# Two attentions in one kernel: the last 64 projected rows of A with high and low weights side by side in one stationary tile

## The chip, the cores and the metric

One core of a Trainium2 chip. The metric is the device time of one execution in microseconds, as the median of several runs. A core has TensorE (PE, with its weight loads PEld), VectorE (DVE), ScalarE (ACT), GpSimd (POOL) and SyncE (SP, which issues most DMAs here). TensorE's products go to eight PSUM banks of 128 partitions x 512 float32; ACT and VectorE read them there, GpSimd works on SBUF alone in this kernel.

## The reference

Two attention blocks of the same size (2048 positions, width 576, 32 heads of 18) stand beside each other in the output: A looks at eight earlier positions in steps of two, B at all.

```python
def _A_ref(x, wqkv, wo):
    qkv = (lambda x, *d: x.transpose(*d))((x @ wqkv).reshape(B, S, 3, H, Dh), 2, 0, 3, 1, 4)
    q, k, v = qkv[0], qkv[1], qkv[2]
    ...
    kg = k[:, :, idx_c, :].reshape(B, H, S, W, Dh)
    vg = v[:, :, idx_c, :].reshape(B, H, S, W, Dh)
    logits = jnp.einsum("bhsd,bhswd->bhsw", q, kg) * scale
    logits = jnp.where(mask[None, None, :, :], logits, -1e9)
    attn = _softmax(logits, axis=-1)
    o = jnp.einsum("bhsw,bhswd->bhsd", attn, vg)
    return (lambda x, *d: x.transpose(*d))(o, 0, 2, 1, 3).reshape(B, S, D) @ wo
...
a = _A_ref(A_x, A_wqkv, A_wo)
b = _B_ref(B_x, B_wqkv, B_wo)
return jnp.concatenate([a, b], axis=-1)
```

The change lies in A's `x @ wqkv`: 1728 output columns (q, k and v of 576 each) for 2048 positions, with a contraction over 576.

## The kernel before

**Products of two parts.** The projections are float32 products made from a high and a low part of each operand: `hi` is the value rounded to `float32r`, `lo` the rest. Each product is taken as high x high, high x low and low x high. `split` (L428) makes both parts: ACT copies to `hi`, another engine subtracts to get `lo`. The contraction of 576 is four pieces of 128 and a last one of 64; for the last, `xhl` holds the high part of x in one half of the partitions and the low part in the other, and the weights stand in both halves (`whh` high, `wll` low, each twice).

**A's projected rows.** The 1728 output columns of A are cut into 14 chunks of 128, chunk 13 having only 64. A chunk's weights are the stationary operand, 512 positions of x move, and the result (128 or 64 rows x 512 positions) is stored to the DRAM tensor `da`, from which A's attention reads q, k and v. `chunk(c)` (L472) makes a chunk's loads (`get`, `get_last`: queue SP) and splits (`put`, `put_last`: ACT, then GpSimd). Two rooms, `a0` for even chunks and `wp` for odd ones from 2 on, each hold one chunk's weights (tiles `ahi`, `alo` of 128x512 and `ahh`, `all` of 128x128). `leave_a` (L713) takes a finished product out: ACT copies the bank to a tile `ohi`, SP stores that to `da`.

**The stream.** `stream` (L344) runs the products of a work list of 92 in groups of four and four turns a group. It cuts each contraction in two halves of the rows: half r=0 uses partitions 0 to 63, half r=1 partitions 64 to 127, and TensorE works on an instruction of each half at the same time. `halves` (L324) lists the pieces of one half: 4 x 3 of the 128-row pieces and one or two of the last, 14 where the half is the one that holds the low rest (`odd`), else 13. In turn 0 of a group half 0 works on product 0 and half 1 on product 1, in turn 1 on 2 and 3; in turns 2 and 3 each half does the other's products into the same banks, so that two halves never write one bank together. After turn 2 products 0 and 1 leave, after turn 3 products 2 and 3. The four banks of the ring "scores" hold a group's products.

**Maxima among the products.** B's softmax needs row maxima of its scores. `maximum` (L240) computes a 128x512 piece of scores on TensorE (L161) into a bank of the ring "else" (three banks) and lets VectorE reduce it (L169). The stream takes 258 such pieces per half along for later. `most(j)` says how many are given out by the end of turn j; `stream` spreads the turn's share evenly over the turn's instructions of each half. Turns 0 to 11 are products for B's v; from turn 12 on the share is 237 pieces in 80 turns. The last turn (j = 91) also carries four scores (L285) of the main part, whose exponentials ACT makes (L293); they use the ring "else" too. The last turn's list begins with them: score, maximum, score in each half.

**Order by hand.** Schedules are lists of functions by turn number: `at(n, ...)` in the projection, run by `slot()` at the end of a turn; chunk k from 4 on is loaded at turn index 36 + 4k - 2 and split at 36 + 4k and 36 + 4k + 1, some four turns ahead of its use. `posts` are small transfers of finished maxima into `qs` (L200, queue SP). The chunks run in the order of the work list: chunks 0 and 1 by pairs of x blocks, then 2 to 13 with all four x blocks, one group each. Chunk 13 is the last group, j = 88 to 91. After the stream comes the main part: 511 steps of four scores, exponentials, maxima for later blocks, and products with v (`weigh`, L763), with A's attention on GpSimd beside them. A bank that is not yet read out makes the instruction that wants to write it wait, and TensorE takes its instructions in order.

Of the kernel before, what the change touches and what calls it, by code (L numbers as in the profile page):

```python
# [7 lines left out]
F32 = mybir.dt.float32  # L8
F32R = mybir.dt.float32r
BF16 = mybir.dt.bfloat16  # L10
AF = mybir.ActivationFunctionType
# [50 lines left out]
def two_attentions(ctx: ExitStack, tc, xa, wa, woa, xb, wb, wob, out):  # L62
# [265 lines left out]
        return [(b[at], a[at]) if weights_move else (a[at], b[at]) for a, b in both]  # L328


    ctx.enter_context(tc.manual_schedule())
    make_set(stack0, 0)

# [10 lines left out]
    def stream(products, most, last):  # L344

        where, ends = {}, {}
        for j in range(len(products)):
            first = j - j % 4
            turn = [((0, 0), (1, 1)), ((0, 2), (1, 3)), ((0, 1), (1, 0)), ((0, 3), (1, 2))][j % 4]
            both = []
            for r, k in turn:
                args, view, _ = products[first + k]
                if j % 4 < 2:  # L360
                    where[k] = view(bank("scores"))
                else:
                    assert sum(given) - ends[k] > 3
                parts = halves(r, *args)
                both.append([(where[k], *ab, j % 4 < 2 and i == 0, j % 4 > 1 and i == len(parts) - 1)
                             for i, ab in enumerate(parts)])
            n = most(j) - given[0]
            others = last if j == len(products) - 1 else ([], [])
            n += 2 if others[0] else 0
            total = n + len(both[0])  # L370
            for r in range(2):
                for i in range(n):
                    both[r].insert((4 * i + 1 + 2 * r) * total // (4 * n), None)
            for pair in zip(*both):
                for r, p in enumerate(pair):
                    if p is None:
                        (others[r].pop(0) if others[r] else maximum(r))()
                    else:
                        ps, a, b, start, stop = p
                        nc.tensor.matmul(ps, a, b, start=start, stop=stop)  # L380
            for k in sorted(k for _, k in turn):
                if j % 4 < 2:
                    ends[k] = sum(given)
                else:
                    products[first + k][2](where[k])
            slot()
            for _ in range(min(len(posts), 2)):
                posts.popleft()()
        do_all(posts)
# [9 lines left out]
    with (tc.tile_pool(name="x", bufs=1, side="right") as xp,  # L399
# [28 lines left out]
        def split(engine, hi, lo, t):  # L428
            nc.scalar.activation(hi, t, AF.Copy)  # L429
            engine.tensor_sub(lo, t, hi)  # L430
# [41 lines left out]
        def chunk(c):  # L472
# [12 lines left out]
                    load(t[1][64 * r : 64 * r + 64, :n], wa[512:, 128 * c : 128 * c + n])  # L485

            def put():
                hi, lo = (a_room(c).tile([128, 512], F32R, name=nm, bufs=1) for nm in ("ahi", "alo"))
                split(nc.gpsimd, hi[:, : 4 * n], lo[:, : 4 * n], t[0][:, : 4 * n])
                w[:2] = ([u[:, n * k : n * k + n] for k in range(4)] for u in (hi, lo))  # L490

            def put_last():
                w[2:] = (a_room(c).tile([128, 128], F32R, name=nm, bufs=1) for nm in ("ahh", "all"))
                split(nc.gpsimd, w[2][:, :n], w[3][:, :n], t[1][:, :n])

            return w, [get, get_last], [put, put_last]

        def a_room(c):
            return a0 if c % 2 == 0 else a1 if c == 1 else wp


# [4 lines left out]
        if True:  # L506
# [195 lines left out]
                    at(gets[c], lambda b=b, c=c: xas[b][1](c))  # L702
                    at(puts[c], lambda b=b, c=c: xas[b][2](c))
            for k in range(2, 14):
                n = 46 if k == 2 else 36 + 4 * k
                if k == 3:
                    at(n, third_rows)
                at(n - 2 if k != 3 else n, *ws[k][1])
                at(n if k != 3 else n + 2, ws[k][2][0])
                at(n if k == 2 else n + 1 if k > 3 else n + 3, ws[k][2][1])  # L710
            at(90, first_room)

            def leave_a(c, b, n, ps):  # L713
                o = xp.tile([128, 512], F32, name="ohi", bufs=4)
                nc.scalar.activation(o[:n], ps, AF.Copy)  # L715
                load(da[128 * c : 128 * c + n, HALO + 512 * b : HALO + 512 * b + 512], o[:n])


            order = [t for i in (0, 8) for j in range(4) for t in (i + j, i + j + 4)]
# [16 lines left out]
                                              lambda ps: ps, lambda ps, i=i, b=b, c=c: leave(i, b, c, ps)))  # L736

            order = [(c, b) for b0 in range(0, NB, 2) for c in range(2) for b in (b0, b0 + 1)]
            order += [(c, b) for c in range(2, 14) for b in range(NB)]
            for c, b in order:  # L740
                n = min(128, 3 * D - 128 * c)
                work_list.append(((b % 2, ws[c][0], xas[b][0], slice(0, n), every),
                                  lambda ps, n=n: ps[:n], lambda ps, c=c, b=b, n=n: leave_a(c, b, n, ps)))

            es = [None] * 4
            few = 7 * (NT - 4) // 4
            turns = len(work_list) - NT + 4
            stream(work_list, lambda j: 7 * (j + 1) // 4 if j < NT - 4 else
                   few - (few - EARLY_PAIRS) * (j - NT + 5) // turns,
                   [[lambda r=r: es.__setitem__(r, score(0, 0, 0, r, "else")), lambda r=r: maximum(r)(),  # L750
                     lambda r=r: es.__setitem__(r + 2, score(0, 0, 0, r + 2, "else"))] for r in range(2)])
        wa_room.close()
# [716 lines left out]
```

## Time and profile before

| | us |
|---|---|
| median of 3 runs | 1582.14 (1580.37 to 1582.5) |
| the profiled execution | 1579.73 |
| its span | 1577.9 |
| TensorE busy / VectorE / ACT / GpSimd | 1569.6 / 1377.1 / 1207.4 / 969.7 |
| the stream's products (L380), first to last start | 81.6 to 409.8 |
| granted TensorE clock | 1.000 |

In rows of instruction groups the columns are: line, engine, operation, out<-in, shapes, count, then busy us and mean ns of one, then the engine's idle time before them and what ended it. In windows: the stretch, its length, busy time of each engine with the count, the granted clock, the share of the DMA engines and GB/s. In the waits: who waited for whom, us in total, times, the longest. In the timeline: start, length, engine, line, operation, tiles, shapes, count, and in brackets the idle time before it. A matmul's or activation's length includes latency, so neighbours overlap: the distance of two starts is what each costs in a row. TensorE counts as busy through nearly all of the stream and the main part; what sets its pace has to be read from counts and distances.

### The profile page before, as it was taken

What the parts mean: (1) busy time and instruction counts of PE and PEld (TensorE: products, weight loads), DVE (VectorE), ACT (ScalarE), POOL (GpSimd) and SP (SyncE); (2) the same over time, 40 slices, a digit from 0 to 9 for tenths busy, and PEclk for the clock granted to TensorE, in tenths of its full rate; (3) what the DMA queues carried; (4) which work ended last, traced back from release to release, by engine and by line L of the source; (5) the groups of instructions that cost most, each with busy time, mean ns of one, the idle gap of its engine ahead of it and who ended that gap; (6) DMA issues with size and microseconds to landing.
All of it is one profiled execution on the core that took longest, in us unless ns stands there. A gap on an engine that the chain in (4) does not pass through costs nothing.

```text
span 1577.9 us, 34942 instructions
## 1 busy us (share of the span) xinstructions
PE 1569.6 (99%) x13272; PEld 966.4 (61%) x13272; DVE 1377.1 (87%) x2333; ACT 1207.4 (77%) x2411; POOL 969.7 (61%) x803
## 2 busy tenths in 40 slices
PE   9999999999999999999999999999999999999998
PEld 7998899999644445445445445444444444545686
DVE  5289999999999999999989999999999999998633
ACT  6424432121799999999999999999999999998654
POOL 2416742210266995995896897897798799682000
PEclk9999999999999999999999999999999999999999
DMA  9948954532312362245325325421721332154311
GB/s 242 240 147 218 270 164 131 138 107 81 62 41 65 73 142 77 64 122 108 75 77 131 89 81 117 120 79 50 149 85 50 91 95 57 51 167 131 140 57 69
DMA packets 188168, 175.65 MB, mean 111 GB/s; under 512 B 119432, under 2 KB 133512, under 8 KB 186272
## 3 DMA queue, kind: packets, MB, share of 16 engines
q1 hardware_dynamic: 182992, 161.73, 37.4%
q0 software_dynamic: 4032, 10.63, 3.3%
q8 instruction: 104, 1.70, 0.5%
q10 hardware_dynamic: 976, 1.07, 0.2%
q14 instruction: 64, 0.52, 0.1%
HBM read 98.77 MB, written 73.47 MB: 109 GB/s over the span
## 4 chain that ended last, share of the span: by engine, by line
PE 93%; DVE 3%; DMA 3%; ACT 1%; SPq 0%; issue 0%; DVEq 0%; ACTq 0%
PE po L766 30%; PE bank L285 19%; PE bank L161 17%; PE bank L380 14%; PE bank L1347 4%; PE bank L1244 3%; PE bank L571 2%; DVE mx L169 2%; PE bank L317 2%; DMA dqk<-ohi 1%; DMA dqk<-olo 1%; DMA qs<-mh 0%; PE bank L1212 0%; ACT e L293 0%; DMA raw<-xa 0%; SPq L530 0%
## 5 line engine op out<-in xcount | busy, mean ns | idle before, releaser
L169 DVE TENSOR_REDUCE mx<-bank 128x2 f32<-128x512 f32 x2048 | 1278.1, 684 | 109.1 <-PE bank L161 81.9
L293 ACT ACTIVATE e<-bank 128x512 f32<-128x512 f32 x2048 | 1047.9, 605 | 80.5 <-PE bank L285 78.0
L161 PE MATMUL bank<-ks,qs 54*128 54x512 f32 (+1 forms) x2464 | 785.8, 380 | 1.6 <-ACT y L1249 0.3
L161 PEld LDWEIGHTS bank<-ks,qs 54*128 54x128 f32 x2464 | 403.2, 184 | 387.6 <-DVE mx L169 341.1
L285 PE MATMUL bank<-qs,ks 56*128 56x512 f32 x2048 | 592.8, 426 | 0.1
L766 PE MATMUL po<-e,v 128*19 128x512 f32 x4096 | 531.7, 599 | 0.5
L285 PEld LDWEIGHTS bank<-qs,ks 56*128 56x128 f32 x2048 | 309.1, 185 | 21.3 <-ACT e L293 14.6
L987 POOL TENSOR_TENSOR pr<-aq,akv 128x1024 f32<-128x1024 f32 x72 | 158.3, 2200 | 16.7 <-PE po L766 13.8
L1029 POOL TENSOR_TENSOR pr<-lg,akv 128x1024 f32<-128x1024 f32 x72 | 158.3, 2198 | 0.6
L766 PEld LDWEIGHTS po<-e,v 128*19 128x19 f32 x4096 | 73.7, 97 | 138.2 <-issue 132.9
L991 POOL TENSOR_TENSOR pr<-pr 128x1024 f32<-128x1024 f32 x64 | 152.6, 2384 | 5.0
L715 ACT ACTIVATE ohi<-bank 128x512 f32<-128x512 f32 (+1 forms) x56 | 30.4, 594 | 149.2 <-issue 134.3
L380 PE MATMUL bank<-xhi,ahi 64*128 64x512 f32 (+1 forms) x448 | 112.9, 386 | 0.0
L380 PE MATMUL bank<-xhi,alo 64*128 64x512 f32 (+1 forms) x448 | 111.7, 387 | 0.0
L380 PE MATMUL bank<-xlo,ahi 64*128 64x512 f32 (+1 forms) x448 | 110.4, 387 | 0.0
L1347 PE MATMUL bank<-wohi,at 64*128 64x288 f32 x480 | 103.3, 305 | 0.0
L1030 POOL TENSOR_TENSOR pr<-pr 128x512 f32<-128x512 f32 x72 | 92.4, 1284 | 5.6
L430 POOL TENSOR_TENSOR alo<-raw,ahi 128x512 fp32r<-128x512 f32 (+1 forms) x14 | 17.6, 1254 | 122.6 <-ACT ahi L429 94.6
L1347 PEld LDWEIGHTS bank<-wohi,at 64*128 64x128 f32 x480 | 74.6, 184 | 27.6 <-ACT e L293 23.8
L525 POOL TENSOR_TENSOR olo<-olo,ohi 128x512 fp32r<-128x512 f32 x36 | 46.2, 1293 | 70.3 <-ACT ohi L524 60.6
L104 POOL CAST mh<-mt 128x32 fp32r<-128x32 f32 x32 | 6.7, 210 | 114.0 <-DVE mt L186 114.0
L1347 PE MATMUL bank<-wolo,at 64*128 64x288 f32 x240 | 70.3, 293 | 0.0
(210 smaller groups left out, 1864.9 us busy)
## 6 DMA issues: line engine op xcount, KB each, us to landing
do<-n SPq DMA_DIRECT2D x30, 512.0 KB
da<-ohi SPq DMA_DIRECT2D x52, 256.0 KB
akv<-da SPq DMA_DIRECT2D x64, 175.5 KB
out<-y SPq DMA_DIRECT2D x31, 288.0 KB
qs<-dqk SPq DMA_DIRECT2D x30, 288.0 KB
ks<-dqk SPq DMA_DIRECT2D x30, 288.0 KB
at<-dao SPq DMA_DIRECT2D x60, 128.0 KB
rec<-drec SPq DMA_DIRECT2D x29, 256.0 KB
```

The costliest lines, as they stand in the source:

```text
L161: return awaiting(nc.tensor.matmul(ps if part is None else ps[:, 256 * r : 256 * r + 256], qs[at, b, p, 128 * t : 128 * t + 128], ks[at, p ...
L169: nc.vector.tensor_reduce(at, ps.rearrange("q (s n) -> q s n", s=2), axis=AX.X, op=ALU.max)
L285: awaiting(nc.tensor.matmul(ps, ks[at, p, 128 * kt : 128 * kt + 128], qs[at, b, p], start=True, stop=True))
L293: nc.scalar.activation(e, ps, AF.Exp, scale=SCALE)
L380: nc.tensor.matmul(ps, a, b, start=start, stop=stop)
L766: nc.tensor.matmul(po[32 * i : 32 * i + 19], vs[g][:, kt, 19 * i : 19 * i + 19], es[i], start=kt == 0, stop=kt == NT - 1)
L987: nc.gpsimd.tensor_mul(pr, ap(st["q"][:, 2 * c], (SUB, 2), (0, W), (1, SUB)), window(st["k"], c))
L991: nc.gpsimd.tensor_add(st["pr"], st["pr"], pr)
L1029: nc.gpsimd.tensor_mul(at, ap(st["lg"], (0, 2), (SUB, W), (1, SUB)), window(st["v"], c))
L1030: nc.gpsimd.tensor_add(at[:, :, :4], at[:, :, :4], at[:, :, 4:])
L1244: nc.tensor.matmul(sums_[r], *both[r][i], start=i == 0, stop=last)
L1347: return nc.tensor.matmul(ps, a, b, start=r == k == 0, stop=r == 1 and k == len(both[1]) - 1)
```

## The change

Chunk 13 has 64 output columns, so its stationary tiles are 64 wide. After the change the high and low weights of that chunk stand side by side in one stationary tile of 128 columns. A piece then has two products (with high x and with low x) where it had three; the high weights' result lands in partitions 0 to 63 of the bank and the low weights' in 64 to 127 (low x low is computed along). Both halves of the bank have to be added: ACT copies one half to its place in `o`, the other to the same rows of a tile `rest`, and GpSimd adds them before the store. The last piece of the contraction is one product instead of one or two.

Chunk 13 changes places with chunk 12 (`a_place`): it is now the last but one group, in room `a0`, and chunk 12 is the last, in room `wp`. Loads and splits follow. `most` is rewritten: the folded turns get two maxima per half each, the other turns share the rest evenly; 258 in all as before.

```diff
+    def folded(r, w, x):
+        both, last = w[:2]
+        at = slice(64 * r, 64 * r + 64)
+        return [(a[at], t[c][at]) for c, a in enumerate(both) for t in x[:2]] + [(last[at], x[2][at])]
...
-                parts = halves(r, *args)
+                parts = folded(r, *args[1:]) if args[0] == "folded" else halves(r, *args)
...
             def put():
+                if folds(c):
+                    t2 = a_room(c).tile([128, 512], F32R, name="ahi", bufs=1)
+                    w[0] = [t2[:, 128 * k : 128 * k + 128] for k in range(4)]
+                    w[2] = a_room(c).tile([128, 512], F32R, name="alo", bufs=1)
+                    split(nc.gpsimd, *(ap(t2[:, n * i :], (2 * n, 4), (1, n)) for i in range(2)), ap(t[0], (n, 4), (1, n)))
+                    return
...
             def put_last():
+                if folds(c):
+                    t2 = w[1] = a_room(c).tile([128, 128], F32R, name="ahh", bufs=1)
+                    split(nc.gpsimd, t2[:, :n], t2[:, n:], t[1][:, :n])
+                    return
...
+        def folds(c):
+            return c == 13
+
+        def a_place(c):
+            return c if c < 12 else 25 - c
+
         def a_room(c):
+            c = a_place(c)
             return a0 if c % 2 == 0 else a1 if c == 1 else wp
...
-                n = 46 if k == 2 else 36 + 4 * k
+                n = 46 if k == 2 else 36 + 4 * a_place(k)
...
             def leave_a(c, b, n, ps):
                 o = xp.tile([128, 512], F32, name="ohi", bufs=4)
-                nc.scalar.activation(o[:n], ps, AF.Copy)
-                load(da[128 * c : 128 * c + n, HALO + 512 * b : HALO + 512 * b + 512], o[:n])
+                at = slice(0, n)
+                if folds(c):
+                    at, other = (slice(64 * r, 64 * r + 64) for r in (b % 2, 1 - b % 2))
+                    rest = ws[c][0][2].bitcast(F32)
+                    nc.scalar.activation(rest[at], ps[other], AF.Copy)
+                    nc.scalar.activation(o[at], ps[at], AF.Copy)
+                    nc.gpsimd.tensor_add(o[at], o[at], rest[at])
+                else:
+                    nc.scalar.activation(o[at], ps[at], AF.Copy)
+                load(da[128 * c : 128 * c + n, HALO + 512 * b : HALO + 512 * b + 512], o[at])
...
-            order += [(c, b) for c in range(2, 14) for b in range(NB)]
+            order += [(c, b) for c in sorted(range(2, 14), key=a_place) for b in range(NB)]
...
-                work_list.append(((b % 2, ws[c][0], xas[b][0], slice(0, n), every),
-                                  lambda ps, n=n: ps[:n], lambda ps, c=c, b=b, n=n: leave_a(c, b, n, ps)))
+                work_list.append((("folded", ws[c][0], xas[b][0]) if folds(c) else
+                                  (b % 2, ws[c][0], xas[b][0], slice(0, n), every),
+                                  lambda ps: ps, lambda ps, c=c, b=b, n=n: leave_a(c, b, n, ps)))
...
-            turns = len(work_list) - NT + 4
-            stream(work_list, lambda j: 7 * (j + 1) // 4 if j < NT - 4 else
-                   few - (few - EARLY_PAIRS) * (j - NT + 5) // turns,
+            folded_ = [args[0] == "folded" for args, _, _ in work_list]
+            plain = [sum(not f for f in folded_[NT - 4 : j + 1]) for j in range(len(work_list))]
+            most = [few + 2 * sum(folded_[:j + 1]) + (EARLY_PAIRS - few - 2 * sum(folded_)) * p // plain[-1]
+                    for j, p in enumerate(plain)]
+            stream(work_list, lambda j: 7 * (j + 1) // 4 if j < NT - 4 else most[j],
```

## The prediction

> **What bounds the kernel now.** I read the page first, then the stage of the change in windows that end where ACT begins to copy a bank out, then that stage's waits, then its last microseconds as a timeline. The page:
>
> ```profile
> span 1577.9 us, 34942 instructions
> PE 93%; DVE 3%; DMA 3%; ACT 1%; SPq 0%; issue 0%; DVEq 0%; ACTq 0%
> L169 DVE TENSOR_REDUCE mx<-bank 128x2 f32<-128x512 f32 x2048 | 1278.1, 684 | 109.1 <-PE bank L161 81.9
> L715 ACT ACTIVATE ohi<-bank 128x512 f32<-128x512 f32 (+1 forms) x56 | 30.4, 594 | 149.2 <-issue 134.3
> ```
>
> TensorE holds 93% of the chain that ended last, so work taken from TensorE should come off the end where TensorE is never kept waiting. Next, the windows restricted to line 380 (`stream`'s products). The first two are one group of four products each, the third is chunk 12, the fourth and fifth are chunk 13's first three turns and its last.
>
> ```profile
> 285.71:300.75 15.04, 15.04 (x110) 14.02 (x110) 1.00 0.64 166
> 300.75:315.55 14.80, 14.80 (x110) 13.86 (x110) 1.00 0.32 100
> ...
> 379.36:394.40 15.04, 15.04 (x111) 13.96 (x110) 1.00 0.21 74
> 394.40:405.95 11.55, 11.55 (x85) 9.45 (x83) 1.00 0.14 48
> 405.95:410.24 4.29, 4.20 (x25) 2.24 (x22) 1.00 0.30 63
> ```
>
> From the code, the two row halves run side by side, and each turn is a row of **slots**: one instruction of each half. A group has 14+14+13+13 = 54 slots of products and, at three maxima per half and turn, 12 more: 66. 15.04/66 = 0.2279 us a slot. The second window is that of a group in which one turn has two maxima per half: 65 slots, and 65 x 0.2279 = 14.81, which is what it took. Two fewer of its 24 reductions would have made it 15.04 x 22/24 = 13.8 if VectorE set the pace. So here **TensorE's slots set the pace**, and VectorE only just follows:
>
> ```profile
> PEld bank L161 <- DVE mx L169: 0.3, 1, 0.3
> 404.57 1.88 DVE L169 TENSOR_REDUCE mx<-bank 128x2 f32<-128x512 f32 x3
> 409.49 1.29 DVE L169 TENSOR_REDUCE mx<-bank 128x2 f32<-128x512 f32 x2 [0.71 <-PE bank L161]
> ```
>
> The waits from 393 to 412 us have TensorE waiting 0.3 us for VectorE. Three reductions in 1.88 us, the last of 0.68, start (1.88-0.68)/2 = 0.60 apart. Six a turn are 3.6 us; a turn is 3.76.
>
> **The change, part by part.** All times are of the profiled execution: 1579.73 us, of which 1577.9 span and 1.83 around it. The runs shown have a median of 1582.14; I take a difference worked out on the one to the other.
>
> *Products.* A folded half has 4 x 2 + 1 = 9 pieces for 13 or 14. With two maxima per half (the new `most`) a folded turn is 11 slots and the group 44. *Maxima.* Their total (258 per half) stays. The old formula gave two instead of three in three of 80 turns: j = 38, j = 65 and the last. The new one gives three in every plain turn but the last, which gets four, so j = 38 and 65 grow by a slot each. *Up to the last turn*, then: old 15.04 + 11.55 = 26.59 us for chunks 12 and 13; new 44 + 2 + 50 (the 17, 17 and 16 slots of chunk 12's first three turns) = 96 slots x 0.2279 = 21.88. **-4.71 us**. Of it 0.16 is that 64-column slots take 11.55/50 = 0.231 us and 128-column ones 0.2279.
>
> The stationary tile gets twice as wide:
>
> ```profile
> L380 PEld LDWEIGHTS bank<-xhi,ahi 64*64 64x64 f32 x31 | 3.7, 132 | 0.2
> L380 PEld LDWEIGHTS bank<-xhi,ahi 64*128 64x128 f32 x38 | 5.7, 186 | 0.0
> ```
>
> The load is 54 ns longer and lies under the other half's and its own previous product: the plain groups pay it in every slot of 0.2279. Were that cover gone, 36 slots x 0.054 = 1.9 us. The Trainium skill's page "TensorE: Matmul & The Clock Gate", section "LDWEIGHTS (loading the stationary operand)", speaks against the change here: a load's time goes with the number of columns, whatever the rows, by its formula 53 ns more for 64 more columns. The two rows agree with it in the difference; a sum that let it show would be 1.9 us higher, and the slots above say that it doesn't show.
>
> *The last turn* changes most. It carries the main part's first four scores (S) among the maxima (M), in the ring of three banks "else". Now:
>
> ```profile
> 405.55 0.54 PE L380 MATMUL bank<-xhi,ahi 64*64 64x512 f32 x2
> ...
> 405.95 1.07 ACT L715 ACTIVATE ohi<-bank 64x512 f32<-64x512 f32 x2 [10.46 <-issue]
> ...
> 406.92 1.07 ACT L293 ACTIVATE e<-bank 128x512 f32<-128x512 f32 x2
> ...
> 407.14 0.69 DVE L169 TENSOR_REDUCE mx<-bank 128x2 f32<-128x512 f32 x1 [0.69 <-PE bank L161]
> 407.56 0.18 PEld L161 LDWEIGHTS bank<-ks,qs 54*128 54x128 f32 x1 [0.48 <-ACT e L293]
> ...
> 407.74 0.28 DVE L179 TENSOR_REDUCE m<-mx 128x16 f32<-128x128 f32 x1
> 408.04 0.18 PEld L285 LDWEIGHTS bank<-qs,ks 56*128 56x128 f32 x1 [0.24 <-ACT e L293]
> ...
> 409.97 0.28 PE L161 MATMUL bank<-ks,qs 54*128 54x256 f32 x1
> ```
>
> It begins at T = 405.55 and the next step at 409.97: 4.42 us for 13 + 4 = 17 slots, which are 3.87; 0.55 is waiting. The order in the ring is S0 S1 M1 M2 S2 S3 M3 M4. M2 needs S0's bank, and S0's exponential queues on ACT behind the two copies of the turn before, until 407.51; hence 407.56, T+2.01. The new last turn has 13 + 6 = 19 slots, 4.33 us, and 12 users of three banks. By the code they stand at slots 0, 2, 3, 5, 7, 8, 10, 11, 13, 15, 16, 18. S0's exponential still ends at T+1.96, so M2, due at 5 x 0.228 = T+1.14, waits until T+2.01: 0.87. Then S2 and S3 go at T+2.5 and 2.7 and M3 at 3.2, and the maxima M3 to M8 come every 0.23 to 0.46 us while VectorE takes one in 0.60. Stepping through with three banks (score to exponential 0.53, exponentials 0.49 apart, maximum to reduction 0.43, bank free at a reduction's end, 0.69), M8 starts at T+5.56 and the turn ends at T+5.79; the same stepping puts the old turn's end at 4.33 against the 4.42 measured, so I add the 0.09: 5.88. **+1.46 us**. Bounds: nothing more than the two slots (+0.46) and, if all of VectorE's eight reductions and the small one follow M2's wait (2.01 + 0.43 + 7 x 0.60 + 0.28, less the old 4.42), +2.5.
>
> *Leaving.* Each folded product is copied by ACT in two halves: eight copies for four, 0.49 us apart (two take 1.07, one 0.59), 2 us more, under the 10.46 us for which ACT was idle before 405.95. A bank is free later, though. With E the end of the third folded turn, copies start at E+0.40; product 1's bank is free at 0.40 + 4 x 0.49 + 0.1 = E+2.46, and the next group first writes it one folded turn later, E + 11 x 0.2279 = 2.51: just in time. GpSimd's sum of two 64x512 halves is not in the trace. Its nearest rows:
>
> ```profile
> L430 POOL TENSOR_TENSOR alo<-raw,ahi 128x256 fp32r<-128x256 f32 x1 | 0.7, 740 | 11.0 <-ACT ahi L429 11.0
> L1030 POOL TENSOR_TENSOR pr<-pr 128x512 f32<-128x512 f32 x72 | 92.4, 1284 | 5.6
> L991 POOL TENSOR_TENSOR pr<-pr 128x1024 f32<-128x1024 f32 x64 | 152.6, 2384 | 5.0
> POOL mh L104 <- DVE mt L186: 29.1, 1, 29.1
> ```
>
> The time goes with the columns, so I take 1.28 (0.74 and 2.38 as bounds). GpSimd does nothing for 29.1 us there. Queued behind the sums are two things. ACT's copy for product 2 reuses the rows of `rest` that the sum for product 0 reads, and product 3's those of product 1: the latter starts at about E + 1.53 + 2 x 1.28 = 4.1 and its bank is free at 5.2, while the second turn of the next group, E + 2.51 + 17 x 0.2279 = 6.39, first needs it. Cover 1.2 us; at 2.38 a sum it would be 1.0 late. SP's stores to `da` wait for the sums, and behind them stand the transfers into `qs` (L200), which belong to blocks that the main part reads only after many steps. Both at 0, up to +1.0.
>
> *Moved.* Chunk 13's load and split take chunk 12's place and the other way round, each a group ahead of its use; the split of chunk 12 (128x512) lands in shorter turns, with 44 slots (10 us) still to go and some 2 us of work. 0.
>
> *Step after the stream.* VectorE comes out of the new last turn with more reductions owed, and the first step needs the banks of M6, M7 and M8. Stepped on, M8's reduction starts at T+6.97 and frees its bank at 7.66; the step's last maximum can go only then, 1.87 after the turn's end. What the step waits for today is ACT, and its last maximum goes beside the score at 411.36, 1.4 after the end:
>
> ```profile
> 410.75 0.57 ACT ohi L715
> 411.36 0.49 PE bank L285
> 411.86 0.99 PE po L766 x8
> ```
>
> The chain goes through the last copy, and that stays put against the end of the stream. I take 0, and keep +0.5. **Sum**: -4.71 + 1.46 = -3.25 us; 1579.73 - 3.25 = 1576.5 for the profiled execution, **1578.9** for the median.
>
> **Rivals.** *The jam goes on* (+0.5 to +1.5): the first step waits for VectorE as well, or ACT's late copies hold a bank in the group after the folded one. For it: the steps behind are TensorE's, so lateness isn't won back. Against: the chain above, and the 1.2 us of cover. -3.25 + 0.9 = -2.35: 1579.8. *No jam*: the exponentials find ACT free, or the ring's order is kinder than my stepping; only the two slots stay: -4.71 + 0.46 = -4.25, 1577.9. Against it: the old turn's 0.55 us, which the stepping gives back within 0.09.
>
> *VectorE is the bound of the stream*, the side where it gets slower. With 0.63 us a reduction (1.88/3) six are 3.78, over a turn's 3.76; then products taken away buy nothing, the number of reductions is the same, and the four put into the last turn cost its +1.46 and the 0.5 behind it: +2.0, 1584.1. It decides from about 0.627 us a reduction (3.76/6). For it: VectorE is never seen idle between the reductions of a plain turn. Against: the 14.80 us group and the 0.3 us of waiting. *The change doesn't do what it says*: the nine pieces are fewer, but the folded turns last as long as their eight copies and four sums, 8 x 0.49 + 2 x 1.28 = 6.5 us beside four turns of 2.5. If copies and sums didn't overlap with the next group, some 3 us of the gain would go: 1581.9.
>
> The page "TensorEngine Tiling" of the Trainium skill, section "PSUM Bottleneck", says that smaller tiles speed up the products but not the emptying of the banks, which may then set the pace; that is this last rival, and of the present kernel the idle 10.46 us of ACT speaks against it.
>
> **How the numbers follow.** About 0.2% (3.2 us) is what a measurement of this kernel tells from no change, and the forecast lies on that line. Chances: forecast 0.42 (its own range 1577.9 to 1580.0; 0.28 of it beyond 0.2%, as the slots are exact and the last turn's upper bound is unlikely), no jam 0.25 (faster), jam goes on 0.18 (within), not what it says 0.07 (within), VectorE 0.08 (its 1584.1 counted as slower, since the runs spread by 2 us). Faster 0.53, within 0.2% 0.39, slower 0.08. The range takes the first three with the spread of the runs, 1580.37 to 1582.5, about one us either way: 1576.8 to 1582.3.
>
> **What would show it.** Right: L380 products of 64*128 only, 36 fewer; a folded group of 10.0 us between ACT's copies with no wait on ACT or GpSimd in it; a last turn of 5.9 us with a wait on `e` of about 0.9 us and then waits on `mx`; the main part unchanged in length. Wrong: folded turns over 2.6 us, a copy waiting for GpSimd with TensorE behind it, plain turns longer than 3.76, or a main part whose first step starts late by more than 0.5.

## The result and the profile after

| | before | changed |
|---|---|---|
| median, us (20 runs each, lowest to highest) | 1581.1 (1578.65 to 1582.62) | 1578.04 (1576.48 to 1580.43) |
| ratio of the two, 95% interval | | 0.9982 [0.9976, 0.9989] |
| span of the profiled execution, us | 1577.9 | 1576.1 |

The kernel became faster by 1.7 to 3.8 us, 3.06 by the medians: on the line of 0.2% where the forecast had put it (1578.9 us). Twelve more runs of the same kernel beside the experiments gave 0.9985 [0.9976, 0.9994], about 2.4 us.

The page of the changed kernel: span and chain. Columns as before.

```profile
span 1576.1 us, 34876 instructions
...
PE 95%; DVE 3%; DMA 1%; ACT 0%; POOL 0%; issue 0%; SPq 0%; DVEq 0%; POOLq 0%; ACTq 0%
```

There are 66 instructions fewer, and TensorE still holds the chain. The stream, cut where ACT starts copies (windows restricted to the products, now line 387): a plain group, the folded group's first three turns, its last turn and chunk 12's first three, and most of the last turn.

```profile
365.15:380.19 15.04, 15.04 (x111) 14.02 (x110) 1.00 0.27 85
380.19:387.66 7.47, 7.47 (x56) 6.96 (x55) 1.00 0.30 99
387.66:401.90 14.24, 14.24 (x102) 12.33 (x101) 1.00 0.19 39
401.90:407.50 5.60, 5.31 (x26) 2.80 (x22) 1.00 0.26 97
```

A plain group still takes 15.04. Three folded turns are 33 slots, 7.52 by the old price and 7.47 measured. The third window has 11 + 50 = 61 slots, 13.90 by that price; it took 0.34 more. I call 380.19 to 401.90 the **first span** (21.71 us; with all 94 slots at 0.2279, 21.42) and what follows, from the copies before the last turn to the first product with v (L800, at 409.69), the **second span**: 7.79 us, where the kernel before has 5.85 (405.95 to 411.80).

The two profiled executions close so: from the copies of A's first product (210.51 before, 211.10 now) to the first product with v they differ by 201.29 - 198.59 = 2.70 us in favour of the change; ahead of that the new one is 0.59 late, 0.23 of it the added slot of turn 38; behind it, 0.29 longer. 2.70 - 0.59 - 0.29 = 1.8, the difference of the spans. From one execution to another of one kernel the parts ahead and behind vary by a microsecond, the piece in between hardly: a second trace of the changed kernel has 198.58 there. Below, that piece is what I read.

The last turn of the changed kernel, from its timeline (rows of TensorE's products and POOL left out):

```profile
401.45 0.39 PE L285 MATMUL bank<-qs,ks 56*128 56x512 f32 x1
...
402.53 0.18 PEld L161 LDWEIGHTS bank<-ks,qs 54*128 54x128 f32 x1 [0.41 <-DVE mx L169]
...
402.87 1.09 ACT L293 ACTIVATE e<-bank 128x512 f32<-128x512 f32 x2
...
403.53 0.18 PEld L161 LDWEIGHTS bank<-ks,qs 54*128 54x128 f32 x1 [0.47 <-ACT e L293]
...
405.33 1.89 DVE L169 TENSOR_REDUCE mx<-bank 128x2 f32<-128x512 f32 x3 [0.58 <-PE bank L161]
...
406.68 0.18 PEld L161 LDWEIGHTS bank<-ks,qs 54*128 54x128 f32 x1 [0.41 <-DVE mx L169]
...
407.33 1.88 DVE L169 TENSOR_REDUCE mx<-bank 128x2 f32<-128x512 f32 x3
...
408.07 0.18 PEld L161 LDWEIGHTS bank<-ks,qs 54*128 54x128 f32 x1 [0.61 <-DVE mx L169]
...
408.66 0.18 PEld L161 LDWEIGHTS bank<-ks,qs 54*128 54x128 f32 x1 [0.41 <-DVE mx L169]
```

The first score starts at 401.45. M1 waits 0.41 us for VectorE, M2 goes at 403.53, T+2.08, behind the exponentials, and later maxima wait for VectorE again; the last two rows belong already to the first step of the main part.

The chain of waits over the same stretch says it in three rows: from 405.33 on it runs through reductions, not products.

```profile
405.33 1.89 DVE mx L169 x3
407.22 0.19 DVE m L179
407.41 0.46 DVE mx L169
```

And the folded products leaving, from the rows of lines by shape between 385 and 396 us (the tile `rest` stands there as `alo`):

```profile
L745 POOL TENSOR_TENSOR ohi<-ohi,alo 64x512 f32<-64x512 f32 x4 | 5.1, 1282 | 5.2 <-ACT ohi L744 4.9
L387 PEld LDWEIGHTS bank<-xhi,ahi 64*128 64x128 f32 x28 | 4.0, 185 | 0.5 <-ACT ohi L744 0.4
```

GpSimd's sum takes 1.28 us. TensorE waits 0.4 us for ACT's last copy of a pair: that is the 0.34 of the third window.

### The profile page after: what moved, and what is told of

It is laid out like the page before. It is cut to its first block, busy times and chain, and to the rows that moved or that the text cites. A ratio compares the mean times of both kernels' runs of the same rounds, so it can differ in the third digit from the quotient of the medians.

```text
span 1576.1 us, 34876 instructions
## 1 busy us (share of the span) xinstructions
PE 1566.0 (99%) x13236; PEld 967.7 (61%) x13236; DVE 1375.7 (87%) x2333; ACT 1210.7 (77%) x2415; POOL 975.9 (62%) x807
## 4 chain that ended last, share of the span: by engine, by line
PE 95%; DVE 3%; DMA 1%; ACT 0%; POOL 0%; issue 0%; SPq 0%; DVEq 0%; POOLq 0%; ACTq 0%
PE po L800 30%; PE bank L285 19%; PE bank L161 18%; PE bank L387 16%; PE bank L1381 4%; PE bank L1278 3%; DVE mx L169 2%; PE bank L595 2%; PE bank L317 2%; DMA dqk<-olo 1%; PE bank L1246 0%; DMA first<-xb 0%; ACT e L293 0%; PE bank L1210 0%; POOL olo L549 0%
## 5 line engine op out<-in xcount | busy, mean ns | idle before, releaser
L285 PE MATMUL bank<-qs,ks 56*128 56x512 f32 x2048 | 591.6, 425 | 0.0
L800 PE MATMUL po<-e,v 128*19 128x512 f32 x4096 | 531.8, 598 | 0.4
L285 PEld LDWEIGHTS bank<-qs,ks 56*128 56x128 f32 x2048 | 308.6, 184 | 20.4 <-ACT e L293 14.5
L800 PEld LDWEIGHTS po<-e,v 128*19 128x19 f32 x4096 | 73.5, 97 | 138.5 <-issue 133.2
L747 ACT ACTIVATE ohi<-bank 128x512 f32<-128x512 f32 x52 | 28.2, 595 | 139.1 <-issue 111.7
L387 PE MATMUL bank<-xhi,ahi 64*128 64x512 f32 x448 | 113.2, 386 | 0.0
L387 PE MATMUL bank<-xlo,ahi 64*128 64x512 f32 x448 | 107.6, 387 | 0.0
L387 PE MATMUL bank<-xhi,alo 64*128 64x512 f32 x416 | 103.0, 387 | 0.0
L437 POOL TENSOR_TENSOR alo<-raw,ahi 128x512 fp32r<-128x512 f32 x13 | 16.9, 1296 | 113.6 <-ACT ahi L436 79.7
```

The lines of the kernel that those rows point to most:

```text
L285: awaiting(nc.tensor.matmul(ps, ks[at, p, 128 * kt : 128 * kt + 128], qs[at, b, p], start=True, stop=True))
L800: nc.tensor.matmul(po[32 * i : 32 * i + 19], vs[g][:, kt, 19 * i : 19 * i + 19], es[i], start=kt == 0, stop=kt == NT - 1)
```

## The experiments

Theory 1: TensorE's slots are the gain; a jam in the last turn (four maxima per half behind scores that hold two of three banks) and a late copy are what it costs. Rivals: VectorE bounds the stream; GpSimd's sums hold the copies; the jam comes from the scores alone.

**Chunk 13 by halves again, all else as changed.**

```diff
-            return c == 13
+            return False
...
-            folded_ = [args[0] == "folded" for args, _, _ in work_list]
+            folded_ = [83 < j < 88 for j in range(len(work_list))]
```

> Chunk 13 by halves again (54 pieces in its group for 36), everything else as in the changed kernel: its place before chunk 12, two maxima per half in its turns, four in the last turn. Two spans are read: from ACT's copies after turn 3 of chunk 11 to those after turn 3 of the last group but one turn (changed kernel: 380.19 to 401.90, 21.71 us), and from there to the first product with v (401.90 to 409.69, 7.79 us). Theory 1 (TensorE's slots are the gain, the jam of the last turn is its loss): 62 slots x 0.231 + 50 x 0.2279 = 25.7 us for the first and 7.8 for the second; against the kernel before it is some 1.5 us slower, since it has the jam (+1.95) and two slots (+0.46) and saves eight of nothing but moved maxima. Theory 2 (VectorE is the bound of the stream, products taken away buy nothing): the first span stays near 21.7, the time is that of the changed kernel.

Measured: ratio to before 1.0011 [1.0002, 1.0020], 1.7 us slower. First span 25.75 us, second 7.80:

```profile
379.98:405.73 25.75, 25.75 (x228) 1.00 0.19 51
```

So 18 slots are worth 4.0 us where TensorE sets the pace, and the rewritten share of maxima with the chunks' new places, without the fold, is a loss. The rival that VectorE bounds the stream falls.

**The old share of maxima with folded products** (three per half in the folded turns, two in the last).

```diff
-            most = [few + 2 * sum(folded_[:j + 1]) + (EARLY_PAIRS - few - 2 * sum(folded_)) * p // plain[-1]
-                    for j, p in enumerate(plain)]
+            most = [few - (few - EARLY_PAIRS) * (j - NT + 5) // (len(work_list) - NT + 4) for j in range(len(work_list))]
```

> The changed kernel with the old share of maxima: three per half in the folded turns, two in the last. Theory (VectorE is the next limit, 0.60 us a reduction): a folded turn has 12 slots, 2.73 us, but six reductions, 3.6 us; the first span (21.71 as changed) grows to about 25.3, the second falls to 5.9, the two slots of j = 38 and 65 go: 1.2 to 1.6 us later than changed at the first product with v, still 0.8 to 1.2 earlier than before. TensorE waits for VectorE in the folded group, about 3 us in all. Rival (VectorE has room): first span 22.3 to 22.7, 1.5 us earlier than changed.

Measured: first span 25.34 us (378.14 to 403.48), second 5.90; 200.09 us from A's first copies to v, 1.5 more than changed and 1.2 less than before; one time of 1578.12. Its folded turns, by lines between 378 and 388 us:

```profile
L169 DVE TENSOR_REDUCE mx<-bank 128x2 f32<-128x512 f32 x18 | 10.8, 677 | 0.0
...
L161 PEld LDWEIGHTS bank<-ks,qs 54*128 54x128 f32 x17 | 3.1, 183 | 2.5 <-DVE mx L169 2.1
```

VectorE is never idle there and TensorE waits for it. VectorE is the **next** limit, at 0.60 us a reduction. With the maxima left where they were, the fold gains 1.2 us up to v; moving them makes it 2.7, and where they go they meet the same engine.

**Two maxima per half in the last turn, four pieces left to the main part.**

```diff
-EARLY_PAIRS = EARLY * NB * PIECES + 2
+EARLY_PAIRS = EARLY * NB * PIECES
...
-            most = [few + 2 * sum(folded_[:j + 1]) + (EARLY_PAIRS - few - 2 * sum(folded_)) * p // plain[-1]
+            most = [few + 2 * sum(folded_[:j + 1]) + min(3 * p, EARLY_PAIRS - few - 2 * sum(folded_))
```

> Two maxima per half in the last turn instead of four; the four pieces taken out are left to the main part (256 per half in the stream instead of 258), all else as changed. Theory 1: the span from the last copies before the last turn to the first product with v falls from 7.79 us to that of the kernel before, about 5.85; what the main part pays for four pieces more is at most 0.5 to 1 us, so 1 to 1.5 us faster than the changed kernel, some 4 us faster than before (ratio about 0.9975). Rival (the jam comes from the scores behind ACT's copies alone, not from the number of maxima): the span falls by the two slots, 0.46, to about 7.3.

The second span fell to 5.89 us, as expected: the jam is the number of maxima. But the time was 1.0020 [1.0011, 1.0030] of before, 6 us over the changed kernel, which neither theory had. From the first to the last product with v the main part took 1163.2 us where the changed kernel has 1155.5. Against the changed kernel's trace, the starts of the steps fall behind by 3.55 us from step 460 to 461, by 1.0 from 461 to 462 and by 2.4 from 495 to 496. The waits of this kernel from 1402 to 1418 us:

```profile
DVE mx L169 <- PE bank L161: 5.4, 3, 3.7
...
PE bank L161 <- DMA drec<-den: 3.4, 1, 3.4
```

There TensorE must have the next block's row maxima, eight small transfers into `qs` (L200) on SP's queue. SP's issues in this kernel, then in the changed one:

```profile
1398.63 0.40 SPq L835 DMA_DIRECT2D do<-n  x1
1399.12 3.07 SPq L200 DMA_DIRECT2D qs<-mh  x4
1403.21 3.89 SPq L200 DMA_DIRECT2D qs<-mt  x4
1407.21 0.35 SPq L845 DMA_DIRECT2D drec<-den  x1
```

```profile
1400.85 2.33 SPq L200 DMA_DIRECT2D qs<-mh  x4
1403.29 3.00 SPq L200 DMA_DIRECT2D qs<-mt  x4
...
1406.83 0.39 SPq L835 DMA_DIRECT2D do<-n  x1
```

With two pieces less in hand a block's maxima are finished two steps later. GpSimd splits them at the same step as ever, 4.7 us after step 455's product with v begins, but on SP the store `do<-n` (512 KB) and a load of weights now stand ahead of the eight transfers instead of behind them: the last is out 13.26 us after that product (1403.21 + 3.89 - 1393.84), in the changed kernel 10.42. I read the wait put down to `drec<-den` as the wait for these transfers, which TensorE is told to await there. The margin at this place is about nothing anyway: four steps from 460 take 8.24 us in the trace of before, 8.65 and 9.13 in two of the changed kernel.

The 1.0 us behind it falls in a stretch in which the granted clock is half. Windows of TensorE (busy time, then clock, DMA share and GB/s), this kernel first, then the changed one:

```profile
1408.80:1412.20 3.40, 3.40 (x19) 0.50 0.91 299
1408.80:1412.20 3.40, 3.40 (x32) 1.00 0.97 259
```

The other kernel with 256 pieces, further down, has such a stretch too (from 1408.0 us on); the kernels with 258 have none here.

The 2.4 us at step 496 are the last block's transfers, which again stand behind stores instead of ahead of them (`out<-y`, 288 KB each); this kernel, then the changed one:

```profile
1497.40 8.76 SPq L1315 DMA_DIRECT2D out<-y  x2
1508.71 2.47 SPq L200 DMA_DIRECT2D qs<-mt  x4
1512.51 0.73 PE L285 MATMUL bank<-qs,ks 56*128 56x512 f32 x4 [2.13 <-issue]
```

```profile
1497.38 2.19 SPq L200 DMA_DIRECT2D qs<-mt  x4
1502.95 10.44 SPq L1315 DMA_DIRECT2D out<-y  x2
```

In this kernel's chain the scores (L285) at 1512.51 follow the landing of the last `qs<-mt` at 1511.36. That the order on SP's queue is the cause is read from the traces of the two kernels with 256 pieces; no run changes that order alone.

**A wide copy**: one copy of 128 rows empties a folded bank, the second copy reads SBUF.

```diff
-                    nc.scalar.activation(rest[at], ps[other], AF.Copy)
-                    nc.scalar.activation(o[at], ps[at], AF.Copy)
+                    nc.scalar.activation(o, ps, AF.Copy)
+                    nc.scalar.activation(rest[at], o[other], AF.Copy)
```

> A folded product leaves its bank by one copy of 128 rows into o; the second copy of ACT takes the other half from o to rest. Same number of ACT instructions, but two read a bank where four did. Theory 1: the wait of TensorE for ACT's copies at the start of the last group (0.4 us) goes, the span from 380.19 to 401.90 (21.71) falls to 94 slots x 0.2279 = 21.4. Rival (the wait is that for GpSimd's sum through rest): it stays, since the sums and their order stay.

First span 21.37 us (379.43 to 400.80), second 7.79. The wait for ACT is gone from the waits of the stretch, with GpSimd's sums still there, so the rival falls.

**No sum.**

```diff
-                    nc.gpsimd.tensor_add(o[at], o[at], rest[at])
```

> GpSimd's sums of the folded products are left out, so the last 64 rows of da hold the high weights' or the low weights' part alone. Theory 1: the sums lie beside other work; the wait of 0.4 us and both spans stay within 0.1 us (21.71 and 7.79). Rival (the sums hold ACT's copies and with them the banks): the first span falls by 0.3 us and ACT's waits for POOL (0.2 us) go.

First span 21.71, second 7.79, and the wait stays:

```profile
PEld bank L387 <- ACT ohi L744: 0.4, 1, 0.4
```

The sums cost TensorE nothing; GpSimd was idle, as the price of nothing in the prediction assumed.

**Both copies of the same rows.**

```diff
-                    nc.scalar.activation(rest[at], ps[other], AF.Copy)
+                    nc.scalar.activation(rest[at], ps[at], AF.Copy)
```

> ACT copies for rest the same rows of the bank as for o, so the two copies of one product have the same partitions on both sides, and the low or high weights' part is added twice. Read is the distance of ACT's folded copies, 0.62 us each in the changed kernel where two plain 64x512 copies stood 0.49 apart before. If a change of partitions on either side keeps two activations from overlapping: 0.49 within a product, 0.62 between products. If it is a wait of one copy for the other (a dependence the program puts there): 0.62 throughout. TensorE's wait of 0.4 us would shrink by some 0.13 to 0.26 in the first case and stay in the second.

ACT's timeline, the changed kernel first:

```profile
387.66 0.59 ACT L743 ACTIVATE alo<-bank 64x512 f32<-64x512 f32 x1 [5.25 <-PE bank L387]
388.28 0.59 ACT L744 ACTIVATE ohi<-bank 64x512 f32<-64x512 f32 x1
388.90 0.59 ACT L743 ACTIVATE alo<-bank 64x512 f32<-64x512 f32 x1
389.51 0.59 ACT L744 ACTIVATE ohi<-bank 64x512 f32<-64x512 f32 x1
```

```profile
387.43 0.59 ACT L743 ACTIVATE alo<-bank 64x512 f32<-64x512 f32 x1 [5.34 <-PE bank L387]
387.92 0.58 ACT L744 ACTIVATE ohi<-bank 64x512 f32<-64x512 f32 x1
388.52 0.59 ACT L743 ACTIVATE alo<-bank 64x512 f32<-64x512 f32 x1
389.02 0.58 ACT L744 ACTIVATE ohi<-bank 64x512 f32<-64x512 f32 x1
```

With the same partitions on both sides the second copy starts 0.49 or 0.50 after the first, inside its 0.59; between products, where the partitions change from 0-63 to 64-127, the distance is 0.60. In the changed kernel each copy differs from its neighbour on one side, and each starts only after the last has ended. The first span was 21.42: the wait went altogether, where I had expected a part. A pair of products is out 2.17 us after its first copy starts (389.02 + 0.58 - 387.43) and not 2.44, and those 0.27 us were nearly all of it.

**Scores later in the last turn**: each half gives a maximum, a score, a maximum, a score, then the rest.

```diff
-                   [[lambda r=r: es.__setitem__(r, score(0, 0, 0, r, "else")), lambda r=r: maximum(r)(),
-                     lambda r=r: es.__setitem__(r + 2, score(0, 0, 0, r + 2, "else"))] for r in range(2)])
+                   [[lambda r=r: maximum(r)(), lambda r=r: es.__setitem__(r, score(0, 0, 0, r, "else")),
+                     lambda r=r: maximum(r)(), lambda r=r: es.__setitem__(r + 2, score(0, 0, 0, r + 2, "else"))] for r in range(2)])
```

> In the last turn each half gives a maximum first, then a score, a maximum, a score, then the other maxima; same instructions, same slots. Theory 1 (the first scores sit in the ring of three banks until ACT has done its copies, and M2 waits for them): the 0.87 us wait goes, the span from the last copies before the last turn to the first product with v falls from 7.79 to about 6.9. Rival (VectorE's eight reductions alone set the end of the turn): it falls by no more than VectorE's idle time before M2's reduction, about 0.6, and stays over 7.2.

Second span 7.40: 0.39 better, not the 0.9 of theory 1. Its waits from 401 to 411 us have no wait of a maximum for `e`, yet

```profile
PEld bank L161 <- DVE mx L169: 2.5, 5, 0.8
```

So the rival is nearer for this question: with eight reductions in the turn and three banks shared with the scores, VectorE's queue sets the end, and the wait for the exponentials, long as it looks in the timeline, costs 0.4.

**The two pieces per half moved to the middle of the stream** (turns 38 and 65 have four, 258 in all).

```diff
-            most = [few + 2 * sum(folded_[:j + 1]) + (EARLY_PAIRS - few - 2 * sum(folded_)) * p // plain[-1]
+            most = [few + 2 * sum(folded_[:j + 1]) + min(3 * p + (p > 26) + (p > 53), EARLY_PAIRS - few - 2 * sum(folded_))
```

> Two maxima per half in the last turn, and the two pieces per half taken out go to two plain turns in the middle of the stream (j = 38 and j = 65 have four); 258 in all. Theory 1 with VectorE just behind TensorE: a turn with four has 17 or 18 slots, 3.9 to 4.1 us, and eight reductions at 0.60, 4.8 us; the three banks take up some of it, so these groups wait 0.3 to 0.6 us each; the end of the stream is as with two in the last turn (5.85). Net 0.8 to 1.3 us faster than the changed kernel up to the first product with v. Rival (there is room in VectorE): no wait in those groups, 15.04 + 0.23 us each, net 1.95 faster. Other rival (VectorE has no room at all): each waits 0.8 or more and nothing is left of the gain.

Second span 5.92; 197.38 us from A's first copies to v, 1.2 less than changed. But those copies come at the end of turn 38, so what a fuller turn 38 costs lies ahead of that piece. ACT's last copy of B's projected rows (L547) and its first of A's, in the changed kernel, then here:

```profile
200.88 0.58 ACT L547 ACTIVATE olo<-bank 128x512 f32<-128x512 f32 x1
...
211.10 1.09 ACT L747 ACTIVATE ohi<-bank 128x512 f32<-128x512 f32 x2 [4.02 <-issue]
```

```profile
200.85 0.58 ACT L547 ACTIVATE olo<-bank 128x512 f32<-128x512 f32 x1
...
211.80 1.09 ACT L747 ACTIVATE ohi<-bank 128x512 f32<-128x512 f32 x2 [4.74 <-POOL xlo L437]
```

With three maxima per half in turn 38 that is 10.22 us, with four 10.95, and 9.99 in the kernel before, which has two there. Counted from B's last copies to v, this kernel is 0.5 us ahead of the changed one (208.33 against 208.82), less than the 0.8 to 1.3 of theory 1. The windows around turn 65:

```profile
303.65:319.16 15.51, 15.51 (x111) 14.07 (x109) 1.00 0.28 91
319.16:334.27 15.11, 15.11 (x112) 14.08 (x110) 1.00 0.30 93
```

That is 0.54 us for a slot of 0.23: this turn costs 0.31 more than its slot, spread over the next group while VectorE catches up, as theory 1 had it. Turn 38 costs 0.5 more than its slot. One time: 1577.29.

**The parts together.** First the wide copy, one maximum ahead of the two scores, and 256 pieces:

> Two maxima per half in the last turn (256 in the stream), each half's list there beginning with a maximum before its scores, and the wide copy of folded products. Theory 1: first span 21.4, second about 5.4; to the first product with v some 2.7 us earlier than the changed kernel, of which the main part takes 0.5 to 1 back for four pieces more: about 2 us faster than the changed kernel and 5 faster than before, ratio to before 0.997. Rival (the main part takes back what the end of the stream gives, since its steps want the same engines): ratio 0.998, as the changed kernel.

First span 21.37, second 5.61, but 1.0017 [1.0008, 1.0026] of before: the main part took 1162.3 us, the same loss as with 256 above. Then with the pieces moved to the middle of the stream:

> Folded as changed, with the two pieces per half of the last turn moved to two plain turns in the middle of the stream (258 in all, none left to the main part), a maximum before the scores in the last turn, and the wide copy. Theory 1 with the prices measured so far: last copies before the last turn to the first product with v 5.6 us (7.79 as changed), the two fuller turns +0.28 and +0.54, the wide copy -0.34: 1.7 us earlier than the changed kernel at the first product with v, and no loss in the main part, since its pieces are the same: 4.1 us faster than before, ratio 0.9974. Rival (main part takes it back, as it did with 256): ratio 0.998 or worse.

> The kernel of e9 once more, since its profiled execution was its slowest (1581.81 us) with 5 us lost ahead of A's chunks. Theory 1 (the 1.75 us that its trace is ahead of the changed kernel between the first A chunk and the first product with v reach the end; the first measurement was short of it by spread): ratio to before 0.9970 to 0.9978. Rival (it is given back elsewhere in most executions): 0.9982 to 0.9990 again, and the trace shows the place: ahead of A's chunks (before keeps 210.5 us to the first of their copies) or behind the first product with v (1166.1 us before, 1166.4 and 1167.0 in the changed kernel's two traces).

> The changed kernel itself beside the others on one chip. Theory 1: ratio to before 0.998, as in its first measurement, and 1.7 us above e9. In its trace 21.7 and 7.8 us for the two spans again; what differs from run to run lies ahead of the stream's A chunks.

| kernel | A's first copies to v, us | B's last copies to v, us | median, us | ratio to before |
|---|---|---|---|---|
| before | 201.29 | 211.28 | | 1 |
| changed, again | 198.58 | 208.80 | 1577.6 | 0.9985 [0.9976, 0.9994] |
| parts together | 196.84 | 207.78 | 1577.09 | 0.9985 [0.9976, 0.9993] |
| parts together, again | 196.80 | 207.73 | 1577.41 | 0.9984 [0.9975, 0.9993] |

The whole is not measurably faster than the changed kernel, and the expected 0.9974 lies just outside both intervals. The piece from A's first copies is 1.75 us shorter both times, but 0.72 of that was paid in turn 38, ahead of it (10.94 us again, where 0.28 had been reckoned), so up to v the gain is 1.0 to 1.1. Another 0.27 lies around the span: the time outside it has a median of 2.11 us in these runs and of 1.83 in the changed kernel's; why is open. What is left, 0.8, is less than these measurements tell apart.

Both profiled executions of this kernel also lose time further ahead: ACT's first copy of a product of the stream's second part (B's projected rows) starts at 121.15 and 121.08 us, in the changed kernel's two traces at 119.09 and 119.19. Windows from 60 us on (busy time of TensorE's products and loads, VectorE, ACT, GpSimd, then clock, DMA share and GB/s), the changed kernel first, then the parts together (their second trace):

```profile
60.00:80.00 20.00, 20.00 (x154) 20.00 (x153) 0.00 (x0) 5.13 (x22) 2.44 (x5) 1.00 0.86 220
```

```profile
60.00:80.00 20.00, 20.00 (x154) 20.00 (x154) 0.00 (x0) 4.55 (x19) 2.09 (x4) 1.00 0.77 185
```

Between 40 and 60 us TensorE has 135 products for 141, and from 60 to 80 the DMAs move less. The edits all lie in later turns, and the kernels of the other experiments start that copy between 118.9 and 119.6. Why this one is late there stays open.

## Why the prediction was right, and where it was not

It forecast 1578.9 us, a little over 0.2% faster; 1578.04 was measured, inside its range. One microsecond of that distance is the starting point, 1582.14 from three runs where twenty have 1581.1: the forecast of -3.25 us stands against -3.06. Step by step:

**Slots.** -4.71 us up to the last turn was worked out at 0.2279 a slot. Measured: the folded turns came to 7.47 for 7.52, the unfolded experiment to 25.75 for 25.7. Right, and with it the readings that TensorE set the pace (the 14.80 us group), that 128-column loads stay covered, and that VectorE is just behind. One row was misread: the 0.3 us for which TensorE waits for VectorE between 393 and 412 us are not in the stream but in the step behind it (below).

**Leaving.** "copies start at E+0.40; product 1's bank is free at 0.40 + 4 x 0.49 + 0.1": here a term was mis-sized. The copies stand 0.62 apart, so the fourth ended 2.44 us after the first began and not 2.06, the bank was free 0.38 later, and "just in time" became 0.34 us of waiting. The price of 0.49 came from two copies with the same partitions; the folded ones change them on one side each time. The sum on GpSimd, 1.28 with nothing behind it, was right, shown by leaving it out.

**The last turn.** +1.46 was forecast, by stepping through three banks. From the first score (401.45) to the next step's first maximum, had it not waited (407.25 + 0.23), it is 6.03 us for 5.88: right within 0.15. The wait that the prediction named first, M2 behind the exponentials, is there, and ends at T+2.08 for T+2.01. But it is not what sets the end: the experiment that takes it away wins 0.39 us, and the one that halves the number of maxima wins 1.9. The eight reductions set it.

**The step after the stream** is the step that failed: "The chain goes through the last copy, and that stays put ... I take 0, and keep +0.5". The chain now goes through reductions, TensorE waits 0.61 and 0.41 us for VectorE in that step, and from the turn's end (407.48) to the first product with v it takes 2.21 us where it took 1.83: +0.38. The kernel before already had a sign of it, beside ACT's copies that the prediction named as what the step waits for:

```profile
410.24 0.18 PEld L161 LDWEIGHTS bank<-ks,qs 54*128 54x128 f32 x1 [0.29 <-DVE mx L169]
```

Reading what a step waits for in the old chain doesn't say what it waits for when another engine comes out of the stage later.

Together: -4.71 + 0.34 + (7.79 - 5.85) = -2.43 us, not -3.25. That is the rival *the jam goes on* (-2.35), whose two places, the step after the stream and ACT's late copies, are both the ones found. The measured ratio's interval (1.7 to 3.8 us) holds both sums and can't tell them apart; the traces do. That the first measurement, -3.06, lies nearer to the forecast is therefore luck; the second measurement gives about -2.4. *No jam* and *VectorE is the bound* fell by the second span and by the unfolded kernel.

**Not foreseen** was that the number of maxima in the stream is tied to a deadline 1000 us later. The change leaves that number at 258, and yet the place shows: step 460 takes 2.40 and 2.91 us in the changed kernel's two traces, 2.04 in the one of before. That is all by which its main part is longer in them (0.3 and 0.9 us); why is open.

## What to carry to other kernels

Before taking work off the engine that sets the pace, add up the next engine for the stage: here TensorE lost 18 slots and VectorE, with 3.6 us of reductions in a turn of 3.76, none of its reductions, so four microseconds saved came with two spent where the reductions were put. Work that is moved between stages can move a queue's order far from it: two pieces per half less cost six microseconds, and as the traces read, small transfers had fallen behind large stores at two places. And a local span has to begin ahead of everything that was edited: the piece read here began just behind a turn that had been made longer, and showed 1.75 us where 1.1 were gained.

## What the runs showed of the hardware

Two 64x512 copies on ACT overlap when both use the same partitions on each side (0.49 us apart at 0.59 each) and don't when a side changes between partitions 0-63 and 64-127 (0.60 to 0.62). The Trainium skill's page "ScalarE: Activation LUTs", section "What ACT_TABLE_LOAD costs", says that ACTIVATEs in a row overlap by about 93 ns; the first distance agrees (0.10), the second shows a case without any overlap. No run says that any change of partitions has this effect: in the wide-copy trace a copy of 128 rows starts 0.54 us after one of 64 rows that took 0.63. The trace of before had a case like the second in its two 64-row copies into `xhl`, one half of the partitions after the other, 0.64 us apart:

```profile
203.75 0.62 ACT L466 ACTIVATE xhl<-raw 64x512 fp32r<-64x512 f32 x1
204.39 0.63 ACT L467 ACTIVATE xhl<-raw 64x512 fp32r<-64x512 f32 x1
```

Stationary tiles of 64x64 cost 0.231 us a slot beside 54x128 ones, against 0.2279 for 64x128, 3 ns a slot more; that the change of width between neighbouring instructions is what costs them is a guess.

The granted clock fell to half in the middle of three traces, for 3.41 us each time: from 1408.8 us on in the trace with two maxima in the last turn (TensorE had stood still for 3.37 us), from 1408.0 in the trace of the parts together with 256 pieces (2.48), and from 191.1 in the first trace of the parts together with 258 (1.88). After the 2.1 us of standing still ahead of 1512.51, shown above, it stayed full, so the length of the wait alone doesn't decide it.
